# Half of the last V tile loaded early, and wo as four rows per partition, in a one-token attention kernel

## The chip, the cores and the metric

The kernel runs on one core of a Trainium2 chip (trn2). Times are device microseconds of that core; the median before the change is 1277.38 us in three runs. The profile also gives the span, from the first to the last traced instruction.

## The reference, cut to what matters

```
x: 1 x 448;  16 query heads, 8 KV heads, 65,536 cached positions, head size 256, bf16
a = softmax(q K^T / 16) V, per head, then @ wo (4096 x 448)     # q = x @ wq
b = ((relu(x @ W_gate)) * (x @ W_up)) @ W_down                  # small
g = sigmoid(sum(x * gate_w));  out = g * a + (1 - g) * b
```

K and V are 8 x 65,536 x 256 bf16 values each, 537 MB of the 549 MB that are read once. There is one token, so nothing is reused: the kernel is a stream of loads, with the arithmetic beside it.

## The kernel before

K and V come in 64 tiles of 8.4 MB (128 partitions of 64 KB), in three buffers, all issued by one queue (SP). A Python list holds the order of the loads; a tile is issued when the last reader of its buffer is done. The end of that list:

```python
        for n in range(1, NT):                      # NT = 32 tiles of K, 32 of V
            order.append(("k", n, TILE))
            if n >= NTH - 1:
                order.append(("v", n - (NTH - 1), TILE))
        NW = H - 3
        order += [("wo", 0, 7.3), ("v", NT - 3, TILE), ("v", NT - 2, TILE)]
        PIECES = [(0, 64), (64, 96), (96, 112), (112, 120), (120, 128)]
        for i, (lo, hi) in enumerate(PIECES):       # the last V tile, in pieces
            order.append(("vp", i, TILE * (hi - lo) / U))
        WO = [(0, 2 * NW), (2 * NW, J - 4), (J - 4, J - 2), (J - 2, J - 1), (J - 1, J)]
        for i in range(1, 5):                       # the rest of wo
            order.append(("wo", i, ...))
        ...
        LASTS = (0, 1, 2, 0, 1, 0)   # buffers of K31, V28, wo, V29, V30, V31
```

V29 takes the buffer of K31, so it can be issued only when the scores of K31 are done. The pieces of V31 take the buffer of V29. wo is loaded with two consecutive rows of 448 values per partition, that is, in runs of 1792 bytes:

```python
                l_["wo", i] = dma("sp", t, "wo%d" % i, lambda e, lo=lo, hi=hi: e.dma_start(
                    wo_sb[:, lo:hi, :, :], A_wo[lo * 256:hi * 256, :].rearrange("(j p s) n -> p j s n", p=128, s=2)),
                    free(("wo", 0)))
```

## Time and profile before

| what | value |
|---|---|
| time, median | 1277.38 us |
| span | 1276.1 us |
| DMA | 430 GB/s, busy in every slice |
| VectorE busy, PE busy | 50%, 33% |
| V29 issued | 1208.27 us |
| last wo load, its 16 landings | 1272.25 to 1273.86 us |

From the page of the kernel before: its span and instructions, the busy share of the DMA engines in 40 slices (9 is 90% or more), and the count of DMA packets.

```profile
span 1276.1 us, 10216 instructions
PE 427.3 (33%) x4568; PEld 167.5 (13%) x4568; DVE 633.2 (50%) x421; ACT 63.3 (5%) x124; POOL 4.6 (0%) x21
...
DMA  9999999999999999999999999999999999999998
...
DMA packets 12948, 549.22 MB, mean 430 GB/s; under 512 B 1283, under 2 KB 3590, under 8 KB 3974
```

The DMA row leaves almost no room, so the work of the DMA engines is the place to look. The end of the chain of waits (start in us, duration, what) shows what follows the last load.

```profile
1241.26 31.47 DMA ring<-in_A_wo_dram
1272.73 0.04 issue
1272.77 1.68 PE A_ps L389 x10
1274.45 0.02 issue
1274.48 0.38 DVE P_sb L582
```

The place that the change aims at is in the timeline of the same kernel (start, duration, engine, line, operation, operands, count). PE finishes the scores of the last K tile, and at that moment SP issues V29.

```profile
1204.63 3.59 PE L378 MATMUL ST<-ring,xc 128*16 128x512 bf16 x32 [5.15 <-PEq L86]
1208.27 0.34 SPq L550 DMA_DIRECT2D ring<-in_A_v_cache_dram  x1
```

The views go no further than this, but the trace holds more. It records every DMA packet with start, duration and size, and every increment of a semaphore. A load adds 16 increments. Those of V28 come one by one 0.3 to 0.6 us after the 16 ends of the DMA engines' last packets of it, so there is one per DMA engine, and the 16 landing times of a load can be listed. For the kernel before, worked out from those records (us; "15th" is the engine before the last):

```
load            first     median    15th      last
V28             1203.18   1204.05   1205.20   1206.13
wo, first part  1209.19   1209.99   1211.07   1211.92
V29             1229.56   1229.88   1230.42   1231.28
V30             1249.02   1249.40   1250.65   1250.72
wo, last part   1272.25   1272.67   1273.77   1273.86
```

The engines are up to 2.9 us apart, and they do not wait for each other. The packets show it: 15 of the 16 engines have begun with wo between 1202.64 and 1204.74 us, while the last one is still on V28 until 1205.63.

### The profile page before, as it was taken

The page shows a single profiled execution, that of the slowest core. Times are in us where ns is not written, and L with a number is a line of the kernel's source. Part 1 is how long each engine was busy: PE and PEld are TensorE (multiplying, and loading weights), DVE is VectorE, ACT ScalarE, POOL GpSimd, SP SyncE. Part 2 cuts the span into 40 slices and gives each one's busy share as a digit, 9 for nine tenths or more (in the row PEclk, how much of TensorE's full clock was granted, in tenths as well). Part 3 has the DMA queues.
Part 4 walks back from the last instruction along what each step waited for, and adds up shares of the span by engine and source line. Part 5 has one row for each costly group of instructions (what it writes and reads, how often), then busy time and mean ns, then how long its engine had stood idle before and what let it go on. Part 6 is the DMA issues. An engine that isn't in the chain of part 4 may idle for free. (4 is left out here: it accounts for less than half of the span.)

```text
span 1276.1 us, 10216 instructions
## 1 busy us (share of the span) xinstructions
PE 427.3 (33%) x4568; PEld 167.5 (13%) x4568; DVE 633.2 (50%) x421; ACT 63.3 (5%) x124; POOL 4.6 (0%) x21
## 2 busy tenths in 40 slices
PE   3633322334123532224331343321333324233254
PEld 1501110111001210002110111110111101011021
DVE  2597633465533655434555444555434655335600
ACT  0001000010000100001000010000100001000000
POOL 1000000000000000000000000000000000000000
PEclk9656666656666575667656666656666656666576
DMA  9999999999999999999999999999999999999998
GB/s 401 448 427 428 436 431 440 433 429 431 436 438 436 428 429 438 436 436 429 429 438 431 438 433 429 433 436 434 436 431 429 436 433 436 433 431 436 405 446 354
DMA packets 12948, 549.22 MB, mean 430 GB/s; under 512 B 1283, under 2 KB 3590, under 8 KB 3974
## 3 DMA queue, kind: packets, MB, share of 16 engines
q1 hardware_dynamic: 12930, 549.03, 99.7%
q8 instruction: 8, 0.13, 0.0%
q14 instruction: 6, 0.05, 0.0%
q10 hardware_dynamic: 4, 0.00, 0.0%
HBM read 549.03 MB, written 0.00 MB: 430 GB/s over the span
## 5 line engine op out<-in xcount | busy, mean ns | idle before, releaser
L367 DVE STREAM_TRANSPOSE ring<-ring 128x2048 uint32<-128x2048 uint32 x256 | 565.4, 2275 | 398.9 <-DMA ring<-in_A_k_cache_dram 398.9
L378 PE MATMUL ST<-ring,xc 128*16 128x512 bf16 x2048 | 222.8, 608 | 745.5 <-PEq L86 745.5
L378 PEld LDWEIGHTS ST<-ring,xc 128*16 128x16 bf16 x2048 | 68.0, 120 | 886.1 <-issue 884.8
L409 PE MATMUL O<-ring,ptp 128*4 128x512 bf16 x2048 | 152.3, 461 | 32.9 <-DMA ring<-in_A_v_cache_dram 18.8
L494 ACT ACTIVATE P_sb<-ST,nmb 128x512 bf16<-128x512 f32 x32 | 45.2, 1412 | 1103.5 <-DVE nmb L492 1103.5
L492 DVE TENSOR_REDUCE nmb<-ST 128x1 f32<-128x512 f32 x32 | 22.1, 689 | 116.8 <-PE ST L378 116.8
L409 PEld LDWEIGHTS O<-ring,ptp 128*4 128x4 bf16 x2048 | 56.9, 100 | 128.1 <-issue 71.8
L419 DVE CAST o_sb<-O 128x512 bf16<-128x512 f32 x8 | 5.5, 692 | 76.8 <-PE O L409 76.8
L513 DVE TENSOR_TENSOR P_sb<-P_sb,hs 128x1024 bf16<-128x1024 bf16 x16 | 18.9, 1222 | 9.4 <-ACT hs L507 9.4
L518 PE MATMUL PT<-identb,P_sb 128*128 128x128 bf16 x128 | 16.2, 307 | 16.8 <-PEq L86 15.8
L459 PE MATMUL M_ps<-xT,ring 128*128 128x1 bf16 x84 | 9.5, 205 | 17.5 <-DMA ring<-in_B_W_up_dram 17.5
L518 PEld LDWEIGHTS PT<-identb,P_sb 128*128 128x128 bf16 x128 | 12.4, 138 | 19.2 <-issue 19.2
L527 ACT COPY ptp<-PT 128x256 bf16<-128x256 bf16 x32 | 10.3, 375 | 23.9 <-PE PT L518 23.9
L341 PE MATMUL QN<-ring,P_sb 128*128 128x512 bf16 x32 | 8.9, 446 | 3.8 <-DMA ring<-in_A_wq_dram 3.8
L459 PEld LDWEIGHTS M_ps<-xT,ring 128*128 128x128 bf16 x84 | 7.2, 152 | 18.1 <-issue 17.7
L494 ACT ACTIVATION_READ_ACCUMULATOR P_sb<-ST,nmb 128x1 f32 x32 | 8.4, 263 | 0.0
L462 PE MATMUL M_ps<-xT,ring 128*64 128x1 bf16 x56 | 7.8, 276 | 0.0
L442 DVE STREAM_TRANSPOSE scr<-P_sb 128x256 uint32<-128x256 uint32 x1 | 0.4, 445 | 13.1 <-ACT P_sb L441 13.1
L503 PE MATMUL M_ps<-identf,hs 128*2 128x128 f32 x8 | 2.5, 308 | 11.1 <-PEq L86 11.1
L539 DVE RECIPROCAL hs<-M_ps 128x2 f32<-128x2 f32 x8 | 1.4, 171 | 8.3 <-PE M_ps L538 8.3
L462 PEld LDWEIGHTS M_ps<-xT,ring 128*64 128x64 bf16 x56 | 5.4, 191 | 0.4
L389 PE MATMUL A_ps<-ring,attnT 128*1 128x224 bf16 x64 | 4.7, 304 | 0.6 <-DMA ring<-in_A_wo_dram 0.6
(74 smaller groups left out, 66.2 us busy)
## 6 DMA issues: line engine op xcount, KB each, us to landing
ring<-in_A_v_cache_dram SPq DMA_DIRECT2D x1, 4096.0 KB, 22.4
ring<-in_A_wq_dram SPq DMA_DIRECT2D x1, 3072.0 KB, 10.4
ring<-in_A_wo_dram SPq DMA_DIRECT2D x1, 2240.0 KB, 38.7
ring<-in_A_v_cache_dram SPq DMA_DIRECT2D x1, 2048.0 KB, 26.9
ring<-in_B_W_down_dram SPq DMA_DIRECT2D x1, 1568.0 KB, 22.0
ring<-in_B_W_gate_dram SPq DMA_DIRECT2D x1, 1344.0 KB, 32.3
ring<-in_B_W_up_dram SPq DMA_DIRECT2D x1, 1344.0 KB, 35.1
ring<-in_A_v_cache_dram SPq DMA_DIRECT2D x1, 1024.0 KB, 28.9
```

Of the source, the lines that this page charges most:

```text
L341: ins = e.matmul(QN_ps, xw3[:, k_, 31 - h:159 - h], rhs, start=(h == 0 and kt == 0), stop=(h == H - 1 and kt == R3))
L367: return lambda e: e.transpose(v, v)
L378: ins = e.matmul(bank[32 * w:32 * w + 16, :], xc[:, x0:x0 + 16], ktv[sl][:, u0:u0 + 16, c, :, r_], start=(b == 0 and c == 0 and r_ == 0), ...
L409: ins = e.matmul(OP[32 * g:32 * g + 4, :], ptp[:, col:col + 13:4], ring[sl][:, k * 512:(k + 1) * 512], start=(a == 0 and k < 4), stop=(a = ...
L419: o1 = op("dv", tn, lambda e: e.tensor_copy(o_sb[:], OP[:]), [pv[n], last.get(("otr", h - 1))])
L459: e.matmul(GU_ps[:, c:c + 1], wf3[which][:, kt * F + ft:(kt + 1) * F:FT], xT[:, kt:kt + 1], start=(kt == 0), stop=False, skip_group_check= ...
L462: ins = e.matmul(GU_ps[64 * half:64 * half + 64, c:c + 1], wfh[which][:, ft:F // 2:FT], xT[:, R3 + half:R3 + half + 1], start=False, stop= ...
L492: smax[n] = op("dv", tk + 22, lambda e, n=n, NM=NM, t_=t_: e.tensor_reduce(NM[:, t_:t_ + 1], ST[n % 2][:], AX.X, ALU.max, negate=True), [q ...
L494: aexp[n] = op("ac", tk + 23, lambda e, n=n, t_=t_, NM=NM, RS=RS: e.activation(P_sb[:, t_:2048:4], ST[n % 2][:], ACTF.Exp, bias=NM[:, t_:t ...
L513: rsc = op("dv", tt, lambda e, X=X, pb=pb: e.tensor_tensor(pb, pb, X[:, 12:16].unsqueeze(1).to_broadcast([128, 256, 4]), ALU.mult), [h7, a ...
L518: ins = e.transpose(PT[rd][:, s * 128:(s + 1) * 128], P_sb[:, (rd * 8 + s) * 128:(rd * 8 + s + 1) * 128], identb[:, :])
L527: ins = e.copy(dst, src)
```

## The change

The intent is twofold. wo of seven KV heads is loaded as four consecutive rows per partition, so that it comes in half as many packets of twice the size (3584 bytes). And the first half of V31, 4 MB, goes into the free end of wo's buffer and is queued right behind the first wo load, so that the DMA engines have work while V29 waits for the scores of K31.

```diff
-        order += [("wo", 0, 7.3), ("v", NT - 3, TILE), ("v", NT - 2, TILE)]
+        order += [("wo", 0, 7.3), ("vp", 0, TILE / 2), ("v", NT - 3, TILE), ("v", NT - 2, TILE)]
...
+        wo4 = ring[slot["wo", 0]][:, 0:J * 2 * D].rearrange("p (h s n) -> p h s n", h=H, s=4)
...    # the output of each head but the last is turned into the new order of rows
+                def f_otr4(e):
+                    for s in range(4):
+                        for q in range(2):
+                            for par in range(2):
+                                ins = e.matmul(T_ps[64 * q:64 * q + 64, s:s + 1], o_sb[:, par * 256 + s:par * 256 + 256:4],
+                                               emat[:, 2 * par + q:2 * par + q + 1], start=(par == 0), stop=(par == 1), ...)
+                def f_norm4(e):
+                    for q in range(2):
+                        ins = e.tensor_scalar(attnT[64 * q:64 * q + 64, h * 4:(h + 1) * 4], T_ps[64 * q:64 * q + 64, :],
+                                              X[64 * q:64 * q + 64, 8 + q:9 + q], None, ALU.mult)
...
-                    sl = slot["vp", 0]
+                    sl, base = (slot["wo", 0], J * 2 * D) if i == 0 else (slot["vp", 1], 0)
...
+                if hi <= J - 2:
+                    dst, src = wo4[:, lo // 2:hi // 2, :, :], A_wo[lo * 256:hi * 256, :].rearrange("(h p s) n -> p h s n", p=128, s=4)
```

More of the change, by code (lines that the diff above doesn't have):

```diff
@@ L237, in bass_gated_mix__gqa_block_cached__glu_gated_reglu__decode_kernel @@
         NW = H - 3
-        order += [("wo", 0, 7.3), ("v", NT - 3, TILE), ("v", NT - 2, TILE)]
-        PIECES = [(0, 64), (64, 96), (96, 112), (112, 120), (120, 128)]
+        order += [("wo", 0, 7.3), ("vp", 0, TILE / 2), ("v", NT - 3, TILE), ("v", NT - 2, TILE)]
+        PIECES = [(0, U // 2), (64, 96), (96, 112), (112, 120), (120, 128)]
         for i, (lo, hi) in enumerate(PIECES):
-            order.append(("vp", i, TILE * (hi - lo) / U))
+            order += [("vp", i, TILE * (hi - lo) / U)] if i else []
         WO = [(0, 2 * NW), (2 * NW, J - 4), (J - 4, J - 2), (J - 2, J - 1), (J - 1, J)]
@@ L259, in bass_gated_mix__gqa_block_cached__glu_gated_reglu__decode_kernel @@
         for kind, i, _ in order:
-            if kind in ("k", "v") or (kind, i) in (("wo", 0), ("vp", 0)):
+            if kind in ("k", "v") or (kind, i) in (("wo", 0), ("vp", 1)):
                 m = r - 3
@@ L400, in free, with make_pv @@
             return out_
-        def make_pv(n, lo, hi, sl, tv, dep):
+        def make_pv(n, lo, hi, sl, tv, dep, base=0):
             h, a = divmod(n, NTH)
@@ L409, in f_pv @@
                     ins = e.matmul(OP[32 * g:32 * g + 4, :], ptp[:, col:col + 13:4],
-                                   ring[sl][:, k * 512:(k + 1) * 512],
+                                   ring[sl][:, base + k * 512:base + (k + 1) * 512],
                                    start=(a == 0 and k < 4), stop=(a == NTH - 1 and k >= U // 2 - 4),
@@ L426, in f_otr @@
                     return ins
-                o2 = mop("pe", tn + 0.5, f_otr, [o1, g_em])
-                o3 = mop("dv", tn + 1, lambda e: e.tensor_tensor(
+                def f_otr4(e):
[3 more added lines that the diff above has]
+                                ins = e.matmul(T_ps[64 * q:64 * q + 64, s:s + 1], o_sb[:, par * 256 + s:par * 256 + 256:4],
+                                               emat[:, 2 * par + q:2 * par + q + 1], start=(par == 0), stop=(par == 1),
+                                               skip_group_check=True)
+                    return ins
+                def f_norm4(e):
+                    for q in range(2):
+                        ins = e.tensor_scalar(attnT[64 * q:64 * q + 64, h * 4:(h + 1) * 4], T_ps[64 * q:64 * q + 64, :],
+                                              X[64 * q:64 * q + 64, 8 + q:9 + q], None, ALU.mult)
+                    return ins
+                o2 = mop("pe", tn + 0.5, f_otr if h == H - 1 else f_otr4, [o1, g_em])
+                o3 = mop("dv", tn + 1, f_norm4 if h < H - 1 else lambda e: e.tensor_tensor(
                     attnT[:, h * 4:(h + 1) * 4].rearrange("p (s q) -> p s q", q=2),
@@ L552, in bass_gated_mix__gqa_block_cached__glu_gated_reglu__decode_kernel @@
                     n, (lo, hi) = NT - 1, PIECES[i]
-                    sl = slot["vp", 0]
-                    dep = dma("sp", t, "vp%d" % i, lambda e, sl=sl, n=n, lo=lo, hi=hi: e.dma_start(
-                        ring[sl][:, lo * 256:hi * 256], v_src(n)[:, lo * 256:hi * 256]), free(("vp", 0)))
-                args = (n, lo, hi, sl, tL[kind, i], dep)
+                    sl, base = (slot["wo", 0], J * 2 * D) if i == 0 else (slot["vp", 1], 0)
+                    assert base + hi * 256 <= U * DH
+                    dep = dma("sp", t, "vp%d" % i, lambda e, sl=sl, n=n, lo=lo, hi=hi, base=base: e.dma_start(
+                        ring[sl][:, base + lo * 256:base + hi * 256], v_src(n)[:, lo * 256:hi * 256]), free(("vp", 1) if i else ("wo", 0)))
+                args = (n, lo, hi, sl, tL[kind, i], dep) if kind == "v" else \
+                    (n, lo, hi, sl, tL[kind, i] if i else tL["v", NT - 3] + 9, dep, base)
                 if ("tev", n // NTH) in last:
@@ L562, in bass_gated_mix__gqa_block_cached__glu_gated_reglu__decode_kernel @@
                 lo, hi = WO[i]
-                l_["wo", i] = dma("sp", t, "wo%d" % i, lambda e, lo=lo, hi=hi: e.dma_start(
-                    wo_sb[:, lo:hi, :, :], A_wo[lo * 256:hi * 256, :].rearrange("(j p s) n -> p j s n", p=128, s=2)), free(("wo", 0)))
+                if hi <= J - 2:
+                    dst, src = wo4[:, lo // 2:hi // 2, :, :], A_wo[lo * 256:hi * 256, :].rearrange("(h p s) n -> p h s n", p=128, s=4)
+                else:
+                    dst, src = wo_sb[:, lo:hi, :, :], A_wo[lo * 256:hi * 256, :].rearrange("(j p s) n -> p j s n", p=128, s=2)
+                l_["wo", i] = dma("sp", t, "wo%d" % i, lambda e, dst=dst, src=src: e.dma_start(dst, src), free(("wo", 0)))
         LAST = last["tn", H - 1]
@@ L573, in bass_gated_mix__gqa_block_cached__glu_gated_reglu__decode_kernel, with f_wo4 @@
                     key = LAST + 2 + 0.1 * i
+                def f_wo4(e, h=h):
+                    for s in range(4):
+                        ins = proj(e, attnT[:, h * 4 + s:h * 4 + s + 1], wo4[:, h, s, :], False, False)
+                    return ins
                 def f_wo(e, h=h, lo=max(lo, 2 * h), hi=min(hi, 2 * h + 2)):
@@ L580, in f_wo @@
                     return ins
-                fin = op("pe", key, f_wo, [l_["wo", i], last["norm", h], l_["dn"]])
+                fin = op("pe", key, f_wo4 if h < H - 1 else f_wo, [l_["wo", i], last["norm", h], l_["dn"]])
         f0 = op("dv", T_END, lambda e: e.tensor_copy(fin_o[:, 0:D2], A_ps[0:1, 0:D2]), [fin])
```

## The prediction

> **What bounds the kernel.** One queue of loads, 549 MB. The page's 40 slices show DMA busy 9 throughout, 430 GB/s; DVE is busy 50%, PE 33%. The chain of waits ends in a 31.47 us wo load, 1.68 us of PE and the output. So only loads count, and of the 16 DMA engines the last to finish: a load's semaphore gets one increment per engine. [...] The trace agrees: the 16 increments of the tile before the first wo load come between 1203.18 and 1206.13 us, those of the last wo load between 1272.25 and 1273.86.
>
> **wo as four rows per partition.** In the packet records 1792 B take 76 to 78 ns and 65,536 B 2422 ns (27.1 B/ns), so 1792 B should take 66. From landings: the first wo load is 80 packets per engine in 5.94 us, 74 ns each; 4096 B packets take 160 ns for 151. So 8 to 9 ns of each are fixed. The change merges 112 packets per engine into 56 of 3584 B: 56 x 8 ns = 0.45 us, 0.32 of it in the first wo load. Every engine carries the same number, so all of it is on the critical path.
>
> **First half of the last V tile behind wo.** Now V tile 29 is issued at 1208.27 us (it waits for the last scores), when the fastest engines have about run out of wo: 14.4 and 11.8 packets in flight (usually 16) at 1208.5 to 1209.5, then slow first packets. Median landing from the first wo load to tile 29 is 19.89 us, against 19.35 for other tiles: a bubble of 0.5 us. 4 MB more queued in front (9.7 us) should close it. But the last engine goes 1211.92 to 1231.28, 19.36 us: it was still on wo and lost nothing. The engine next to it lost nothing either, and lost 0.88 us later, about when a 16 KB instruction fetch ran (1241.6). The bubble falls on engines that end early, so closing it is worth about 0, and only widens the spread of the last landings.
>
> **Moved and added, off the path.** V tile 29 lands 9 us later; the rest of tile 31 is issued after its 6.5 us of PE work, near 1247, with 12 us of tile 30 in flight as now. The moved half's PE work runs in an idle wait. Per head but the last: 16 tiny matmuls for 4 and one more 0.16 us DVE operation; loads have over 20 us of queued lead. The end stays.
>
> **Predicted:** 1277.4 - 0.45 = 1276.9 us, 8 times in 10 between 1276.1 and 1277.4; faster by over 2% 0.005, within 2% 0.99, slower 0.005.
>
> **What would show it.** First wo load: median landing 5.6 us after the tile before; no dip of packets in flight at V tile 29; the early engines' last landing about 1 us earlier, the last engine's only 0.45, so the final load's spread grows from 1.6 to about 2.1 us. Tail unchanged.
>
> **What would make it wrong.** Instruction fetches take DMA time on single engines (0.9 us seen). PE's program grows, so a fetch may fall on another engine: if the late engine is spared, the bubble's 0.5 us shows too; if hit, the gain is gone. Or 3584 B packets may carry more fixed time than 4096 B ones.

## More of the kernel before

VectorE transposes each K tile in place in eight instructions, before PE computes its scores:

```python
        def f_trans(sl, w):
            v = ring[sl][:, w * 4096:(w + 1) * 4096].bitcast(U32)
            return lambda e: e.transpose(v, v)
        ...
                tr = [op("dv", tk + 2.22 * w, f_trans(sl, w), [kd]) for w in range(8)]
```

## The result, and the profile after

The kernel is correct. Its median is 1277.23 us in 6 runs (1277.18 to 1277.41), against 1277.41 us for the kernel before (1277.26 to 1278.05). The ratio is 0.9998, with a 95% interval from 0.9985 to 1.0011: the same. A ratio here is the mean time of one kernel's fast runs over that of the other's of the same rounds, so it is not quite the ratio of the medians quoted. The measured time lies in the predicted range, but it is 0.18 us under before and not 0.45.

The spans tell more than the times. Every one of the six runs with the change has a span of 1275.5 to 1275.7 us; the kernel before has 1275.9 to 1276.8 in all 27 runs taken later beside the experiments. The page of the kernel with the change:

```profile
span 1275.5 us, 10391 instructions
PE 423.9 (33%) x4652; PEld 169.6 (13%) x4652; DVE 635.1 (50%) x428; ACT 63.4 (5%) x124; POOL 4.3 (0%) x21
...
DMA packets 12052, 549.22 MB, mean 431 GB/s; under 512 B 1283, under 2 KB 1798, under 8 KB 3078
```

There are 896 packets fewer, 56 per engine, as counted beforehand. The end of its chain of waits names an earlier wo load than before, but what follows the very last landing is as long: 2.2 us to the end of the span in both (1273.86 to 1276.06 before, 1273.30 to 1275.51 after).

```profile
1247.82 23.29 DMA ring<-in_A_wo_dram
1271.11 0.04 issue
1271.15 0.90 PE A_ps L390 x8
1272.05 0.20 PE M_ps L425 x4
1272.25 1.66 PE A_ps L390 x16
1273.90 0.03 issue
1273.93 0.38 DVE P_sb L607
```

V29 is issued at nearly the same time as before; the timeline of the kernel with the change has

```profile
1204.52 3.59 PE L379 MATMUL ST<-ring,xc 128*16 128x512 bf16 x32 [5.16 <-PEq L86]
1208.14 0.33 SPq L565 DMA_DIRECT2D ring<-in_A_v_cache_dram  x1
```

The landings, from the trace's records:

```
load            first     median    15th      last
V28             1203.04   1203.79   1205.03   1205.99
wo, first part  1208.69   1209.43   1210.67   1211.63
V31, half       1218.40   1219.15   1220.38   1221.36
V29             1237.75   1238.50   1239.73   1240.71
wo, last part   1270.43   1271.79   1272.35   1273.30
```

Three things are as predicted. The first wo load takes 5.64 us at the median (5.94 before), for a 3584-byte packet takes 142 ns at the median. The pause at V29 is gone: the packets in flight stay above 16 from 1208 to 1211 us, where they were 14.4 and 11.8. The last landing is 0.56 us earlier; from V28 on, which leaves out what differed at the start, it is 0.42 us (67.73 to 67.31). In the profile before, the engine that is last on V28 is not the one that is last at the end, as experiment 3 will show, so the 0.42 us is not the gain of one engine.

One thing is not. The time fell less than the span. Time minus span is 1.3 us for the kernel before (1277.35 and 1276.1 in the profiled run) and 1.7 us for the kernel with the change (1277.24 and 1275.5). Something outside the traced span costs 0.4 us more.

So there were two questions. Which part of the change gave the shorter span? And where did the other 0.4 us come from?

My theory was that of the prediction: one late engine sets the end, the pause at V29 does not touch it, and so the wider rows give all of the gain and the moved half nothing. The rival was that the pause counts. For the time outside the span, the candidates were the wo layout, PE's longer program and VectorE's longer program.

### The profile page after: what moved, and what is told of

Its sections match the earlier page's. It is cut to its first block, busy times and chain, and to the rows that moved or that the text cites. A ratio compares the mean times of both kernels' runs of the same rounds, so it can differ in the third digit from the quotient of the medians.

```text
span 1275.5 us, 10391 instructions
## 1 busy us (share of the span) xinstructions
PE 423.9 (33%) x4652; PEld 169.6 (13%) x4652; DVE 635.1 (50%) x428; ACT 63.4 (5%) x124; POOL 4.3 (0%) x21
## 5 line engine op out<-in xcount | busy, mean ns | idle before, releaser
L368 DVE STREAM_TRANSPOSE ring<-ring 128x2048 uint32<-128x2048 uint32 x256 | 565.4, 2275 | 395.2 <-DMA ring<-in_A_k_cache_dram 395.2
L410 PE MATMUL O<-ring,ptp 128*4 128x512 bf16 x2048 | 147.7, 450 | 36.3 <-PEq L86 23.7
L432 PE MATMUL M_ps<-emat,o_sb 128*64 128x1 bf16 x112 | 4.5, 199 | 6.6 <-PEq L86 6.6
L439 DVE TENSOR_SCALAR attnT<-M_ps,hs 64x4 bf16<-64x4 f32 x14 | 3.1, 220 | 6.3 <-PE M_ps L432 6.2
```

What stands on the lines that cost most here:

```text
L410: ins = e.matmul(OP[32 * g:32 * g + 4, :], ptp[:, col:col + 13:4], ring[sl][:, base + k * 512:base + (k + 1) * 512], start=(a == 0 and k < ...
```

## The experiments

Twelve kernels ran, in three groups of four. All gave correct outputs. A first form of the kernel with seven added memsets was found to have a race, because the memsets wrote the same bytes without waiting for each other; in the form that ran each has its own columns. In each group the kernel before ran nine times beside them. Each group ran on another chip, so numbers of different groups are compared with that reserve.

| run | time, median | span, median (range) | time - span | last landing, profiled run |
|---|---|---|---|---|
| before, group 1 | 1277.60 | 1276.3 (1276.0 to 1276.7) | 1.30 | |
| control, before | 1277.51 | 1276.2 (1276.1 to 1276.4) | 1.31 | 1274.06 |
| moved half alone | 1277.38 | 1276.1 (1276.0 to 1276.2) | 1.28 | 1273.87 |
| four rows alone | 1277.81 | 1276.1 (1275.9 to 1276.6) | 1.68 | 1274.00 |
| control, both | 1277.29 | 1275.6 (1275.5 to 1275.7) | 1.69 | 1273.41 |
| before, group 2 | 1277.43 | 1276.1 (1276.0 to 1276.8) | 1.31 | |
| both, short VectorE program | 1276.10 | 1274.7 (1274.5 to 1274.8) | 1.32 | 1272.58 |
| before, short VectorE program | 1276.41 | 1275.1 (1275.1 to 1275.2) | 1.31 | 1273.01 |
| before, V29 later | 1280.82 | 1279.5 (1279.3 to 1279.5) | 1.39 | 1277.08 |
| both, V29 later | 1277.33 | 1275.6 (1275.5 to 1275.7) | 1.73 | 1273.44 |
| before, group 3 | 1277.53 | 1276.2 (1275.9 to 1276.7) | 1.31 | |
| both, 433 instructions | 1277.33 | 1276.0 (1275.5 to 1276.9) | 1.29 | 1273.59 |
| before, 440 instructions | 1277.75 | 1276.1 (1276.0 to 1276.5) | 1.65 | 1274.26 |
| before, PE program longer | 1277.51 | 1276.2 (1276.0 to 1276.9) | 1.40 | 1273.99 |
| both, 568 instructions | 1278.38 | 1276.6 (1276.5 to 1277.4) | 1.70 | 1275.15 |

### 1. Control: the kernel before

> The kernel before, unchanged, as a control. Every theory expects a ratio of 1.0000; what it shows is the scatter against which an effect of 0.45 us (0.035%) has to be read, and the scatter of the span beside the scatter of the time.

The ratio was 0.9999 (0.9986 to 1.0013). The ratio of times cannot decide about 0.45 us. The spans scatter as much as the times (1276.0 to 1276.7 against 1277.32 to 1277.99 in this group), but they leave out what happens outside the span, and the profiled last landings of a kernel repeat to 0.2 us (1273.86 and 1274.06).

### 2. The moved half alone

```diff
-                o2 = mop("pe", tn + 0.5, f_otr if h == H - 1 else f_otr4, [o1, g_em])
+                o2 = mop("pe", tn + 0.5, f_otr, [o1, g_em])
...    # and the same for the normalisation, for f_wo4 and for the wo loads: two rows again
```

> Only the first half of the last V tile is moved behind the first wo load; wo keeps two rows per partition. Theory (the last of 16 DMA engines sets the end, and the pause before V tile 29 falls on engines that end early): no packet of tile 29 starts late, first engine's landing of the last wo load about 1 us earlier, last engine's unchanged, span 1276.1 within 0.2. Rival (the pause before tile 29 is on the critical path, its mean of 0.5 us counts): last landing and span 0.5 us shorter.

Last landing 1273.87 us against 1274.06 of the control and 1273.86 of the first profile; span 1276.1. The first engine's landing of the last wo load came at 1271.08 instead of 1272.44. The theory holds: early engines gain 1.4 us, the end gains at most 0.2.

### 3. Four rows alone

```diff
-        order += [("wo", 0, 7.3), ("vp", 0, TILE / 2), ("v", NT - 3, TILE), ("v", NT - 2, TILE)]
+        order += [("wo", 0, 7.3), ("v", NT - 3, TILE), ("v", NT - 2, TILE)]
...
-                    sl, base = (slot["wo", 0], J * 2 * D) if i == 0 else (slot["vp", 1], 0)
+                    sl, base = slot["vp", 0], 0
```

> Only wo goes to four rows per partition; the order of the loads stays. Theory: the first wo load's median landing follows the tile before by 5.6 us instead of 5.94; the pause before V tile 29 grows by about 0.3 us for early engines; the last engine loses nothing there, so last landing and span are 0.45 us shorter, the same as with the whole change. Rival (the pause counts): the gain of the packets in the first wo load is eaten by a longer pause, and the end moves by 0.13 us at most (the packets of the two later wo loads).

Here my theory fell. The first wo load was faster (5.60 us at the median), and the late engine did gain: from V28 to V29 its landings go 1206.07, 1211.62, 1230.97, without a pause. Yet the last landing was 1274.00, no better than the control, and the span 1276.1. The rival expected this number.

The packet records show why. On one engine, a packet starts where the one before ended (in the kernel before, each of 8173 starts between 100 and 1200 us lies within 5 ns of the end before it, and behind five fetches within 14 ns), so the stream of large packets can be sorted into 16 engines, and the few packets that fetch instructions fall into place among them. In this kernel a fetch of 16 KB of PE's instructions at 1241.9 us takes 0.94 us of one engine, and the V30 packet behind it takes 2.91 us instead of 2.42. That engine loses 1.43 us. (That the fetch is PE's is read from its time: in the kernel before and in its forms of experiments 5 and 8 it comes after the same 4412 recorded matmuls.) It was one of the early engines, but the pause had already taken its lead:

```
engine's first V29 packet and end of its V30, us; L = late engine, P = engine with the PE fetch
                   L start   L end      P start (its first packet)   P end
before             1211.46   1250.16    1209.59 (2.92 us)            1250.26
control, before    1211.75   1250.45    1209.44 (3.00 us)            1250.19
four rows alone    1211.16   1249.85    1209.33 (3.52 us)            1250.58
```

A packet of this size takes 2.42 us in a running stream. So the kernel before has not one last engine but two that end within 0.3 us of each other. L is cured by the smaller wo load only. P is cured by closing the pause only. With four rows alone, P starts V29 when V29 is issued, however early it was done with wo, and ends 0.7 us behind L. P is not alone in its long first packet: in the kernel before, V29's issue ended at 1208.61 us and its first packet started at 1209.23, 0.62 us later; on the nine engines that began it first, up to 1209.65, the first packet took 2.92 to 3.23 us, on the other seven 2.42 to 2.53.

### 4. Control: both

> The kernel with the change, unchanged, on this chip with the others. Theory: span 0.45 to 0.6 us under before, last landing of the final wo load about 0.45 us earlier; time of the same size if the part outside the span is equal, else the difference is lost in the scatter.

Span 1275.6 and last landing 1273.41. The moved half alone gives 0.1 to 0.2 us of span, four rows alone 0.1 to 0.2, and both together 0.6 to 0.7. The first two lie inside the scatter of the spans; the third does not. In the kernel with the change the PE fetch comes at 1251.9 us, and its engine ends V30 at 1258.26, while L ends at 1259.59: P is out of the race.

### 5 and 6. A later issue of V29

```diff
-                    dep = dma("sp", t, "r%d" % sl, lambda e, sl=sl, n=n: e.dma_start(ring[sl][:], v_src(n)), free(("v", n)))
+                    dep = dma("sp", t, "r%d" % sl, lambda e, sl=sl, n=n: e.dma_start(ring[sl][:], v_src(n)),
+                              free(("v", n)) + ([last["f", H - 1]] if n == NT - 3 else []))
```

> The kernel before, V tile 29 issued 3.4 us later (it waits in addition for ScalarE's factors of the last head, at about 1211.6). Theory: now every engine runs dry, the late one too; tile 29 lands on all engines about 3.4 us later than the early ones did (first 1229.6 to 1233.0), the late engine loses about 1.8 us, and the engine with the PE page ends last: span 2.7 to 3.5 us longer (1276.2 to 1279.3). Rival (a pause costs by its mean, or nothing): 3.4 us at the median engine but only 1.8 at the end, or none.

> The kernel with the change and the same later issue of V tile 29. Theory: 4 MB of V tile 31 stand in front of it (9.7 us), so no engine runs dry: span as with the change, 1275.6 within 0.2. Rival (the later issue delays the chain of tiles itself): as much longer as the kernel before.

Both came as the theory said, though V29 was issued at 1211.29 us, 3.0 us later and not 3.4. The kernel before is 3.4 us longer in span (1279.5 against 1276.1): P is the last engine again; it starts V29 at 1212.42 us with a first packet of 3.24 us and ends V30 at 1253.47, 3.2 us later than before. All engines now begin V29 within 0.4 us (1212.26 to 1212.65), the spread of its landings falls from 1.72 us to 0.56, and the last landing goes from 1211.86 (wo) to 1233.10, 21.24 us where a tile takes 19.36: now the late engine loses too, up to 1.88 us. With the moved half in the queue a delay of 3.2 us (issue at 1211.35) costs nothing (1275.6). That is what the moved half buys: slack for the issue of V29, an estimated 9.7 us (the time that this load takes: 1209.43 to 1219.15 at the median landings above), of which 3.2 were tested.

### 7. Both, with a shorter VectorE program

What makes L late? In all six traces at hand by then, sorted into engines, L carries three 8 KB fetches of a queue that loads instructions (`q14 instruction` on the page), and no other engine carries more than one fetch before V28. In the kernel with the change these are at 58.4, 417.4 and 865.9 us. Each takes 0.325 us, and the next packet takes 3.08 us instead of 2.42: 0.98 us per fetch, 2.95 us in all, which is the spread seen. VectorE has issued 47, 170 and 317 instructions by then, 123 and 147 apart, so these should be pages of VectorE's program (in experiment 12, with four such fetches, they are 127 to 130 apart). The experiment shortens VectorE's program and leaves the loads alone:

```diff
-            v = ring[sl][:, w * 4096:(w + 1) * 4096].bitcast(U32)
+            v = ring[sl][:, w * 16384:(w + 1) * 16384].bitcast(U32)
...
-                tr = [op("dv", tk + 2.22 * w, f_trans(sl, w), [kd]) for w in range(8)]
+                tr = [op("dv", tk + 8.88 * w, f_trans(sl, w), [kd]) for w in range(2)]
```

> The kernel with the change, with each K tile's eight VectorE transposes issued as two of four times the width: VectorE's program is 192 instructions shorter, its work is the same. Theory (the last DMA engine sets the end, and it is last because it alone carries VectorE's instruction pages: 8 KB fetches at 58, 417 and 866 us, each 0.98 us of that engine): one fetch fewer in the run, the late engine's lead over the next shrinks from 0.95 us to about 0, last landing and span about 0.9 us shorter than with the change alone (span 1275.6 to 1274.7). Rival (that engine is slower for another cause): fetches move, the end does not.

The page of this kernel has 192 VectorE instructions fewer, and the same data transposed, a little faster (554.0 us in all against 565.4; 17.3 us instead of 17.7 from start to end for K31):

```profile
span 1274.8 us, 10199 instructions
PE 429.3 (34%) x4652; PEld 170.5 (13%) x4652; DVE 623.7 (49%) x236; ACT 63.3 (5%) x124; POOL 4.6 (0%) x21
...
L368 DVE STREAM_TRANSPOSE ring<-ring 128x8192 uint32<-128x8192 uint32 x64 | 554.0, 8691 | 400.4 <-DMA ring<-in_A_k_cache_dram 400.4
```

In the kernel with the change the same line of the page is

```profile
L368 DVE STREAM_TRANSPOSE ring<-ring 128x2048 uint32<-128x2048 uint32 x256 | 565.4, 2275 | 395.2 <-DMA ring<-in_A_k_cache_dram 395.2
```

The fetches moved with VectorE's program: 128.8 and 867.6 us on L, 0.98 us each, and no third one. The last landing is 1272.58 us, 0.7 to 0.8 us earlier than in the two profiles of the kernel with the change, and now 0.16 us behind the 15th engine. The span is 0.9 us shorter, as expected. The faster transposes let V29 be issued earlier (1207.08), but experiment 6 showed that this kernel does not depend on that. The rival is out.

This is the version that beats both kernels: 1276.10 us against 1277.43 for the kernel before in the same group. The ratio is 0.9988 (0.9974 to 1.0002), but no span of its five runs (up to 1274.8) comes near one of the nine of before (from 1276.0).

### 8. The kernel before, with the shorter VectorE program

> The kernel before with the same shorter VectorE program. Theory (two engines end nearly together: the one with VectorE's pages, untouched by the pause before V tile 29, and one that lost to the pause and then carries a PE page near 1241 us at 1.4 us): only the first gets better, so span 1276.2 to about 1276.1, 0.3 us at most. Rival (the VectorE-page engine alone sets the end of both kernels, as predicted before the change was run): 0.9 us shorter here too.

The theory missed: the span fell by 1.0 us, to 1275.1, not by 0.3. My sum had left the pause as it was. The timeline of this kernel shows that it was not:

```profile
1203.43 3.59 PE L378 MATMUL ST<-ring,xc 128*16 128x512 bf16 x32 [4.97 <-PEq L86]
1207.06 0.34 SPq L550 DMA_DIRECT2D ring<-in_A_v_cache_dram  x1
```

V29 is issued 1.2 us earlier than in the kernel before (1208.27). The scores of K31 wait for K31, and K31 is complete when its last engine has delivered. The late engine is 1 us less late (one fetch of 0.98 us fewer), and K31 lands 0.84 us earlier (1185.91 against 1186.75). The other 0.36 us are the wider transposes, which take 17.30 us for K31 instead of 17.66. So the scores are ready earlier, V29 is issued earlier, and the pause shrinks: the first landing of V29 is 1228.54 instead of 1229.56. L and P both gain: they end V30 at 1249.41 and 1249.34, where they ended at 1250.16 and 1250.26. How much of P's gain comes from the late engine and how much from the faster transposes was not separated. The late engine had been counted once, as the end; it also sets the issue of V29.

### 9 to 11. The time outside the span

> The kernel with the change, with two of the eight VectorE transposes merged into one in seven of the 32 K tiles, so that VectorE's program has 433 instructions as before the change, not 440. The two kernels with four rows per partition and 440 instructions spend 1.7 us of the measured time outside the traced span, all others 1.3. Theory (the extra 0.4 us belongs to the length of VectorE's program): outside part back to 1.3 us, span still 1275.6, so time about 1276.9. Rival (it belongs to the wo layout or to PE's longer program): time stays at 1277.25.

> The kernel before with seven tiny VectorE memsets added, 440 instructions. Theory (length of VectorE's program): outside part 1.7 us, span 1276.2 as before, time 0.4 us longer than before, about 1277.9. Rival: no change, 1277.5.

> The kernel before with the 12 small matmuls per head that the change adds to PE's program, here without use. Theory (VectorE's program): outside part stays 1.3 us, span 1276.2, time 1277.5. Rival (PE's program): outside part 1.7 us, time 1277.9.

```diff
     # both, 433 instructions: in seven K tiles the first two transposes are one
+                tr = [op("dv", tk + 2.22 * w, f_trans(sl, w, 2 if n < 7 and w == 0 else 1), [kd])
+                      for w in range(8) if not (n < 7 and w == 1)]
     # before, 440 instructions: a memset of 2 unused columns in each of seven K tiles
+                for _ in range(1 if n < 7 else 0):
+                    op("dv", tk + 22.05, lambda e, c=next(padc): e.memset(padv[:, c:c + 2], 0.0))
     # before, PE program longer: 12 unused matmuls per head but the last
+                    for s in range(12):
+                        ins = e.matmul(M_ps[:, 484:486], o_sb[:, 0:256:2], emat[:, 0:2], start=True, stop=True)
```

Seven idle memsets are enough: with 440 VectorE instructions the kernel before spends 1.65 us outside the span (1.62 to 1.70 in five runs), and the kernel with the change, cut back to 433, spends 1.29 (1.28 to 1.34). With 440 the kernel before takes 0.22 us more time (1277.75 against 1277.53), not the 0.4 expected; its median span happened to be 0.1 us shorter. PE's longer program adds at most 0.1 (1.28 to 1.44), and the kernel with V29 later, whose PE program is unchanged, has 1.39 too. Over all kernels, the medians are 1.28 to 1.40 us with 433, 248 or 241 VectorE instructions and 1.65 to 1.73 with 440 or 568. So the 0.4 us belongs to VectorE's program, and not to wo or to PE.

The traces also show where it falls, for they record increments of semaphores after the end of the span. The last of these comes 1.42 to 1.52 us after the span's end in the eight profiled runs with at most 433 VectorE instructions, and 1.77 to 1.88 us after it in the six with 440 or 568. The last nine increments are of one semaphore. Between the fifth and the sixth of them pass 0.10 us in those eight runs and 0.45 to 0.47 us in these six. So the extra time is a wait after the kernel's last instruction. Which engine waits there and for what, where the step between 433 and 440 lies, and why there is none between 440 and 568, stays open.

The expected time of 1276.9 was not reached: the five runs with 433 instructions have spans from 1275.5 to 1276.9, with a median of 1276.0, though the profiled one lands its last wo load at 1273.59, within 0.3 us of the two profiles of the kernel with the change. The best of the five took 1276.84. The scatter on this chip leaves the sum of the two effects unproven; each of them is shown.

### 12. Both, with 128 instructions more

```diff
+                for _ in range(8 if n == 0 else 4 if n < NT - 1 else 0):
+                    op("dv", tk + 22.05, lambda e, c=next(padc): e.memset(padv[:, c:c + 2], 0.0))
```

> The kernel with the change with 128 tiny VectorE memsets added in VectorE's idle time (one 8 KB page of instructions, under 8 us of VectorE work spread over 31 tiles). Theory (the engine with VectorE's pages is the last one): one more fetch on that engine during the run, last landing and span 0.98 us longer, 1275.6 to 1276.6, and the other engines' landings unchanged. Rival (fetches do not set the end): span 1275.6.

The median span is 1276.6, 1.0 us more than with the change on the first group's chip (1275.6), as expected. The expectation took 128 instructions for one page; the traces before it had shown 123 and 147 from fetch to fetch, and here they are 127 to 130. L now carries four fetches, at 59.3, 299.7, 600.7 and 906.5 us, 0.98 us each; the median engine's last landing is 1271.80, where it was 1271.79. The profiled run was the slowest of the five (1277.4); why it was 0.8 us slower than the median one I did not find. In its trace L is late by more than its fetches: with 0.98 us taken off for each, it lands V28 0.1 us before the median engine, and 0.4 to 0.9 us before it in the other profiles.

## Why the prediction was right or wrong

- **What bounds the kernel** was right: the end is set by the last of 16 DMA engines. Experiments 7 and 12 move that one engine by a page of instructions less and a page more, and the end follows by 0.9 and 1.0 us.
- **The cost of a packet** was near: 8 to 9 ns of fixed time were forecast, and a packet of 3584 bytes took 142 ns (132 at the 27.1 B/ns of the 65,536-byte packets), so 10. What the late engine gains was forecast too large. In the control of the kernel before, where that engine is also the last at the end, it takes 67.65 us from V28 to the end, and in the two profiles of the change 67.31 and 67.30: a gain of 0.34 us, not 0.45. Its first wo load fell only from 5.81 us to 5.64 and 5.65, by half of the forecast 0.32; the median engine gained 0.30 there.
- **"Every engine carries the same number, so all of it is on the critical path"** failed as it stood. Alone, the wider rows gave 0.1 to 0.2 us of span (experiment 3). An engine that finishes wo earlier and then waits for V29 has gained nothing.
- **"The engine next to it lost nothing either"** is the step behind that error. I took the 15th landing of one load and the 15th of the next for the same engine. The lists are sorted, so the ranks are not engines. The packet records show that the engine which lost 1.43 us at 1241.6 was one of those that had paused at V29 (its first packet took 2.92 us). It ended V30 at 1250.26, after the late engine with 1250.16.
- **"Closing it is worth about 0"** was right for the moved half alone (0.1 to 0.2 us) and wrong for the change: without it the gain of the wider rows would not have come out. The gain of the pair is not the sum of its parts, since each part cures one of two engines that end together.
- **The spread** of the last wo load grew to 2.87 us, not 2.1. I had used the median pause (0.5 us); by the first landings it was 1.0 (20.37 us from wo to V29, a tile being 19.35).
- **"A fetch may fall on another engine"** had the risk right and its nature wrong for VectorE: its pages did not wander. In every trace that could be sorted without doubt they fell on one engine, the late one, at 0.98 us each (in a few traces two engines cross within nanoseconds and cannot be told apart after that).
- **The total** of 1276.9 missed 1277.23 by 0.33 us because a term was absent: seven VectorE instructions more cost 0.4 us outside the traced span. The span itself gained 0.6 us, a little more than the forecast. That the time came out near the forecast is partly luck. The rows' gain came out only because the moved half, rated at 0, closed the pause; the late engine's own gain was 0.34 us; the rest of the 0.6 is not explained (that engine delivered V28, before wo began, up to 0.4 us earlier in the two profiles of the change); and 0.4 us were lost outside the span.

## What to carry to other kernels

When the DMA engines are busy all the time, as here (9 tenths or more in 39 of 40 slices), ask which of them ends last, and why it is late; follow engines by their packets, not by their rank in a sorted list. Here two engines that end together hid each other: curing one alone showed 0.1 to 0.2 us of span, inside the scatter, and curing both 0.6 to 0.7. So parts of a change have to be tried together as well as alone. Instructions are loads too (0.98 us of one DMA engine for each 8 KB fetch of VectorE's): here, fewer and larger VectorE instructions took more off the time (1.1 to 1.2 us with the change, of which 0.4 lies outside the span, and 1.0 without) than both parts of the change together (0.2 to 0.3).
